# Chunked attention and two feed-forward layers on one core: first products in three sub-steps, one four-bank accumulator tile, a new order

## The chip, the cores and the metric

The engines are PE (matrix products, and PEld, its loading of the stationary operand), DVE (vector), ACT (scalar, with a table for exp), POOL (here mostly the issuer of outgoing transfers) and SP (issuer of all incoming transfers). Each engine works its instructions off in the order in which they stand and waits at semaphores for the others.

## The reference, cut to what matters

Attention: 4 batches, 8 heads, 768 positions, head size 64. A chunk of 32 queries sees 8 memory keys, 16 keys to the left, its own 32 and 8 to the right, 64 in all:

```python
scores = scale * np.matmul(q_c, k_full.transpose(0, 1, 3, 2))
scores = scores - np.max(scores, axis=-1, keepdims=True)
a = np.exp(scores)
a = a / (np.sum(a, axis=-1, keepdims=True) + 1e-09)
out[:, :, c_start:c_end] = np.matmul(a, v_full)
```

The 3072 tokens of 512 values then go through two layers of 512 -> 2048 -> 512:

```python
h = x @ w_in;  g = s * np.maximum(h, 0.0) ** 2 + b;               x = g @ w_out
h = x @ w_in;  g = np.maximum(h, 0.0) + alpha * np.minimum(h, 0.0);  y = g @ w_out
```

The weights come as 64-bit floats. Every product of the two layers is made of three: each operand is split into a high and a low part, and high x low, low x high and high x high are added up in PSUM.

## The kernel before, in words

**Tiles and blocks.** The tokens are 24 tiles of 128 (a tile is 128 positions of one batch, all heads) and 6 blocks of 512 (4 tiles). The hidden 2048 values are 16 slices `f` of 128. A **unit** is one layer, one block `j` and one slice `f`: step `g1` makes the hidden slice (12 products of 128x128 by 128x512 into bank `ph`), ACT and DVE apply the activation and split the result into `gh` and `gl`, and `g2` adds its part of the output into the four PSUM banks `po` (again 12 products). The first three slices of block 0 are done in two halves of 256 tokens (`HALVES`), so the first half can begin when two tiles of attention are done. `g2` of a unit stands two units (`LAG`) behind its `g1`.

**Order of the units.** Blocks 0 and 1 run first through slices 0 to `SEG`-1, put their sums by in DRAM (`spill`), then go through the other slices and add. So the early part needs only the first `SEG` weights for two blocks. After them come blocks 2 to 5, then layer 2, all slices at a time.

**Attention.** Per tile: scores (`scores`, products named `sc`, or `sp` where a tile's scores and the former tile's values share a step `products`), row maxima, exp, row sums, reciprocals and scaling on DVE and ACT (`softmax`), a turn by PE (`pt` or `turns`), a copy to SBUF (`aT`), the products with the values (`px`, `sp`), and the split into `xh` on ACT and `xl` on DVE. Tiles in `BY_HEAD` take exp head by head with the sum as a by-product of ACT, the others in one instruction with the sum on DVE. Tiles 0 to 3 (`ALONE`) use the `po` banks in pairs, tile 0 and 2 one pair, 1 and 3 the other; later tiles use the pair `pa`. A score or value product of 32 instructions in the program runs as 64 products in the trace.

**Weights.** `convert` turns the raw 64-bit words of slice `f` into two 32-bit parts: magnitude (ACT), clamp, shift, low, sign (DVE), high part (ACT), rest (DVE). Slices 0 and 1 are loaded and converted with the two matrices apart (`w0i`, `w0o`, ...).

**What sets the order.** All steps are handed to `Plan` with a cost, a rank and what they wait for; `Plan.order` lists them by time of a model of the engines, the loads and the fetching of PE's own instructions, and the instructions are emitted in that order. The model's constants and the tables at the head of the file (`FIRST_LOADS`: order of the first loads on SP; `TILE_RANKS`, `CONV_RANKS`, `STEPS`: ranks) decide only the order; nothing of them is executed. `Pace` models PE: its `BLOCK` is a block of 256 instructions that has to be fetched, `due` when the next one is there.

## Time and profile before

| what | value |
|---|---|
| three runs | 1143.62, 1147.26, 1149.77 us |
| the profiled execution's own time | 1147.76 us |
| its span, first to last instruction | 1146.0 us |
| PE busy | 1117.8 us (98%) |
| DVE, ACT, POOL busy | 607.9, 350.9, 28.8 us |
| mean granted clock of PE | 0.995 |
| DMA moved | 98.32 MB, mean 86 GB/s |

The page of the profile gives busy times, 40 slices of the span, the chain that ended last and the costliest groups; other views used are the waits of one engine (who waited for whom), the timeline (instructions in order of time, like ones merged, the idle time before each group in brackets) and the table of windows (busy time of each engine in a stretch, with the granted clock). A line number such as L605 is that of the kernel before; the kernel after has other numbers.

### The profile page before, as it was taken

The page shows a single profiled execution, that of the slowest core. Times are in us where ns is not written, and L with a number is a line of the kernel's source. Part 1 is how long each engine was busy: PE and PEld are TensorE (multiplying, and loading weights), DVE is VectorE, ACT ScalarE, POOL GpSimd, SP SyncE. Part 2 cuts the span into 40 slices and gives each one's busy share as a digit, 9 for nine tenths or more (in the row PEclk, how much of TensorE's full clock was granted, in tenths as well). Part 3 has the DMA queues.
Part 4 walks back from the last instruction along what each step waited for, and adds up shares of the span by engine and source line. Part 5 has one row for each costly group of instructions (what it writes and reads, how often), then busy time and mean ns, then how long its engine had stood idle before and what let it go on. Part 6 is the DMA issues. An engine that isn't in the chain of part 4 may idle for free.

```text
span 1146.0 us, 18300 instructions
## 1 busy us (share of the span) xinstructions
PE 1117.8 (98%) x7848; PEld 926.0 (81%) x7848; DVE 607.9 (53%) x942; ACT 350.9 (31%) x615; POOL 28.8 (3%) x58
## 2 busy tenths in 40 slices
PE   4799999999999999999999999999999999999998
PEld 4788888888888888888887788888888888888886
DVE  6796945454544445434799844434433434344333
ACT  5675734332223223224565311111111111111111
POOL 0000000000000000000000000000000000000000
PEclk9899999999999999999999999999999999999999
DMA  9918013423113113004557102002002002000000
GB/s 345 351 38 302 10 66 110 146 82 125 51 42 138 42 42 134 1 1 170 198 184 255 76 1 101 10 1 94 17 1 92 19 1 89 23 1 4 34 1 37
DMA packets 46241, 98.32 MB, mean 86 GB/s; under 512 B 4944, under 2 KB 4944, under 8 KB 46160
## 3 DMA queue, kind: packets, MB, share of 16 engines
q1 hardware_dynamic: 40320, 77.22, 19.4%
q0 software_dynamic: 5696, 19.93, 4.6%
q8 instruction: 61, 1.00, 0.4%
q14 instruction: 20, 0.16, 0.0%
q10 hardware_dynamic: 144, 0.01, 0.0%
HBM read 76.16 MB, written 20.97 MB: 85 GB/s over the span
## 4 chain that ended last, share of the span: by engine, by line
PE 49%; issue 42%; DMA 3%; DVE 3%; POOL 1%; ACT 1%; SPq 0%; POOLq 0%; DVEq 0%; ACTq 0%
PE ph L605 24%; PE po L666 22%; PE po L664 2%; DMA raw<-in_win_dram 1%; POOL x1d L703 1%; DVE a L309 1%; DMA spill<-os 1%; DVE a L314 1%; DMA qT<-in_qt_dram 0%; PE sp L488 0%; DMA qa<-in_qt_dram 0%; DMA vd<-in_vw_dram 0%; DVE w L327 0%; DVE gl L649 0%; DMA x1d<-o 0%
## 5 line engine op out<-in xcount | busy, mean ns | idle before, releaser
L605 PE MATMUL ph<-xh,w 128*128 128x512 f32 (+1 forms) x1560 | 509.7, 389 | 1.6 <-issue 0.9
L605 PEld LDWEIGHTS ph<-xh,w 128*128 128x128 f32 x1560 | 293.7, 189 | 61.7 <-DVE g L636 1.1
L605 PE MATMUL ph<-xl,w 128*128 128x512 f32 (+1 forms) x780 | 302.0, 387 | 0.0
L644 ACT ACTIVATE gh<-g 128x512 fp32r<-128x512 f32 (+1 forms) x195 | 121.7, 624 | 465.8 <-DVE g L636 385.2
L664 PE MATMUL po<-gh,w 128*128 128x512 f32 (+1 forms) x792 | 257.9, 387 | 0.2 <-DVE o L688 0.2
L666 PE MATMUL po<-w,gh 128*128 128x512 f32 x768 | 251.6, 389 | 0.5 <-DVE o L700 0.5
L649 DVE TENSOR_TENSOR gl<-g,gh 128x512 fp32r<-128x512 f32 (+1 forms) x195 | 133.1, 683 | 101.7 <-ACT gh L644 100.2
L631 DVE TENSOR_SCALAR g<-ph,cst_sb 128x512 f32<-128x512 f32 x96 | 72.0, 750 | 213.2 <-PE ph L605 213.1
L664 PEld LDWEIGHTS po<-gh,w 128*128 128x128 f32 x792 | 148.7, 189 | 30.1 <-DVE o L688 0.7
L605 PEld LDWEIGHTS ph<-xl,w 128*128 128x128 f32 x780 | 147.6, 189 | 28.6
L666 PEld LDWEIGHTS po<-w,gh 128*128 128x128 f32 x768 | 144.1, 188 | 31.0 <-DVE o L700 1.2
L664 PE MATMUL po<-gl,w 128*128 128x512 f32 (+1 forms) x396 | 152.1, 384 | 0.0
L666 PE MATMUL po<-w,gl 128*128 128x512 f32 x384 | 149.4, 389 | 0.0
L616 ACT ACTIVATE g<-ph 128x512 f32<-128x512 f32 (+1 forms) x99 | 57.8, 584 | 137.7 <-PE ph L605 134.2
L664 PEld LDWEIGHTS po<-gl,w 128*128 128x128 f32 x396 | 75.0, 189 | 14.1
L623 DVE TENSOR_TENSOR g<-g 128x512 f32<-128x512 f32 x48 | 33.2, 692 | 97.0 <-ACT g L616 96.9
L666 PEld LDWEIGHTS po<-w,gl 128*128 128x128 f32 x384 | 72.1, 188 | 14.9
L627 DVE TENSOR_SCALAR g<-g,cst_sb 128x512 f32<-128x512 f32 (+1 forms) x99 | 52.6, 531 | 42.6 <-ACT g L621 41.3
L636 DVE SCALAR_TENSOR_TENSOR g<-ph,g 128x512 f32<-128x512 f32 x96 | 66.3, 690 | 2.9
L296 ACT ACTIVATE a<-raw 128x1024 f32<-128x1024 f32 (+1 forms) x36 | 37.6, 1045 | 22.6 <-DVE w L327 14.3
L321 ACT ACTIVATE w<-a 128x1024 fp32r<-128x1024 f32 (+1 forms) x36 | 34.8, 967 | 31.2 <-DVE a L314 30.1
L327 DVE TENSOR_TENSOR w<-a,w 128x1024 fp32r<-128x1024 f32 (+1 forms) x36 | 39.5, 1100 | 1.2 <-ACT w L321 1.2
(83 smaller groups left out, 517.6 us busy)
## 6 DMA issues: line engine op xcount, KB each, us to landing
raw<-in_win_dram SPq DMA_DIRECT2D x64, 256.0 KB, 4.7
raw<-in_wout_dram SPq DMA_DIRECT2D x64, 256.0 KB, 5.3
x1d<-o POOLq DMA_DIRECT2D x24, 512.0 KB, 3.4
vd<-in_vw_dram SPq DMA_DIRECT2D x40, 256.0 KB, 4.1
kd<-in_kw_dram SPq DMA_DIRECT2D x20, 368.0 KB, 5.0
xh<-x1d SPq DMA_DIRECT2D x6, 1024.0 KB, 5.6
xl<-x1d SPq DMA_DIRECT2D x6, 1024.0 KB, 7.6
qT<-in_qt_dram SPq DMA_DIRECT2D x20, 256.0 KB, 3.9
```

Source lines behind the costliest of these rows:

```text
L296: nc.scalar.activation(out=temp["a"], in_=words(1).bitcast(F32), func=ACTF.Abs)
L321: nc.scalar.activation(out=w[:, :, 0, :], in_=temp["a"], func=ACTF.Copy)
L327: nc.vector.tensor_sub(out=w[:, :, 1, :], in0=temp["a"], in1=w[:, :, 0, :].bitcast(F32))
L605: nc.tensor.matmul(p, lhsT=w[:, a, kk * P:(kk + 1) * P], rhs=x[:, kk, cols], start=(i == 0), stop=(i == 3 * KD - 1))
L616: nc.scalar.activation(out=new_g(u), in_=ph.pop(u), func=ACTF.Relu)
L627: nc.vector.tensor_scalar(out=g, in0=g, scalar1=cst_sb[:, 0:1], scalar2=cst_sb[:, 1:2], op0=ALU.mult, op1=ALU.add)
L631: nc.vector.tensor_scalar(out=new_g(u), in0=ph[u], scalar1=0.0, scalar2=cst_sb[:, 2 + f:3 + f], op0=ALU.min, op1=ALU.mult)
L636: nc.vector.scalar_tensor_tensor(out=g, in0=ph.pop(u), scalar=0.0, in1=g, op0=ALU.max, op1=ALU.add)
L644: nc.scalar.activation(out=gh, in_=gt[u], func=ACTF.Copy)
L649: nc.vector.tensor_sub(out=gl, in0=gt.pop(u), in1=gh.bitcast(F32))
L664: nc.tensor.matmul(po[d][:, cols], lhsT=w[:, a, ds_], rhs=g, start=start, stop=stop)
L666: nc.tensor.matmul(po[d], lhsT=g[:, ds_], rhs=w[:, a, :], start=start, stop=stop)
```

## The change

**First products in three sub-steps.** `g1` takes a list of kinds, and whether it is the first and the last of its bank. For layer 0, blocks 0 and 1 and slices below `APART` = 6 it is planned as three steps of four products: high x high needs the high part of the weight and the tiles' `xh` alone, low weight x high needs the rest of the weight, high x low needs `xl`. All other units keep one step of twelve, ordered kind by kind per quarter as before.

**One accumulator tile.** The four `po` banks are one tile for the whole kernel, not a new tile for each segment and each lone tile; tiles 0 to 3 get a view of two of its banks, so maxima, subtraction and the two splits of such a tile are one instruction, not two.

**Order.** `SEG` goes from 7 to 8, tile 3 takes exp by head too, the tables of ranks and of first loads have new numbers, and the model's load rate and instruction fetch have new constants (a block is asked for 48 instructions into the one before).

```diff
-SEG = 7
+SEG = 8
 LAG = 2
 HALVES = 3
+APART = 6
...
-FIRST_LOADS = """q0 q1 w1i v0 q3 w0o q2 v2 w0i v1 w1o q4 v3 w2 w3 w4 v4 w6 q5 v7 q6 v5 q7 w5 w9 v6 w7 w8""".split()
+FIRST_LOADS = """q0 q1 w1i v0 q3 w0i q2 v1 w0o v2 w1o q4 w2 w3 q5 v3 w7 v5 w4 w6 q6 v7 v4 w5 v6 w9 w8 q7""".split()
...
-BY_HEAD = (1, 2, 4, 5, 6)
+BY_HEAD = (1, 2, 3, 4, 5, 6)
...
-STEPS = (28, 18, 18, 47, 43, 38)
+STEPS = (59, 89, 62, 132, 93, 79)
...
-    BLOCK, FIRST = 256, 184
+    BLOCK, FIRST, AHEAD = 256, 184, 48
...
+            if block >= 0 and into == self.AHEAD:
                 self.due[block + 1] = t + fetch(t)
...
-    RATE = 396e3
+    RATE = 382e3
...
-    FETCH = 2.7, 5.3
+    FETCH = 1.6, 5.1
...
+    po_all = psum.tile([P, KD, BLK], F32, name="po")
+    po = [po_all[:, d] for d in range(KD)]
...
         if i in ALONE:
-            return [psum.tile([P, 2, HP, D], F32, tag=f"po{2 * ALONE[i] + par}", name=name) for par in range(2)]
+            both = po_all[:, 2 * ALONE[i]:2 * ALONE[i] + 2].rearrange("p b (two a n) -> p b two a n", two=2, a=HP)
...
+        each = [(kk, a, (xh, xl)[b][n]) for kk in range(KD) for a, b in kinds]
+        for i, (kk, a, x) in enumerate(each):
+            nc.tensor.matmul(ph[u], lhsT=w[:, a, kk * P:(kk + 1) * P], rhs=x[:, kk, cols],
+                             start=first and i == 0, stop=last and i == len(each) - 1)
...
+        if layer == 0 and j < 2 and f < APART:
+
+            his = [x_hi[j * TPB + t] for t in range(cols.start // P, cols.stop // P)]
+            s = plan.add("PE", 4 * mm, rank, lambda: g1(u, ((0, 0),), True, False), his + [conv_high[f], id_, in_turn[0]],
+                         takes=("ph", ("ph", u)), count=8)
+            rest = [(((1, 0),), [conv_done[layer, 0, f]]), (((0, 1),), xs)]
+            for n_, (kinds, needs) in enumerate(rest if f == 0 else rest[::-1]):
+                s = plan.add("PE", 4 * mm, rank, lambda kinds=kinds, n_=n_: g1(u, kinds, False, n_ == 1), [s, *needs], count=8)
```

**What moves.** Three places matter for the prediction. In the rows, `x32` or `x4` is the number of like instructions in a row; 32 score or value products run as 64.

The first place is the start of ACT's list, before (lines of the kernel before):

```order
L727 DMA cst_sb<-in_cst_dram 128x18
L296 ACT_TABLE_LOAD
L296 ACTIVATE a<-raw 128x512
L433 ACTIVATE e<-e 128x512
L452 ACTIVATE e,rs<-sc,nm 128x64 x6
```

and now:

```order
L724 DMA cst_sb<-in_cst_dram 128x18
L435 ACT_TABLE_LOAD
L435 ACTIVATE e<-e 128x512
L301 ACTIVATE a<-raw 128x512
L454 ACTIVATE e,rs<-po,nm 128x64 x6
```

The exp of tile 0 (`e<-e`) stood behind the first weight's magnitude (`a<-raw`); it now stands ahead of it, and the table's loading is the exp's.

The second place is PE from tile 1's values on (`px<-aT,vd`), before:

```order
L488 MATMUL px<-aT,vd 64x32 x32
L401 MATMUL sp<-kd,qT 32x64 x32
L401 MATMUL sc<-kv,qa 32x64 x32
L605 MATMUL ph<-xh_74,w 128x256
L605 MATMUL ph<-xl_76,w 128x256
L605 MATMUL ph<-xh_74,w 128x256 x2
```

and now:

```order
L490 MATMUL po<-aT,vd 64x32 x32
L606 MATMUL ph<-xh_74,w 128x256 x4
L409 MATMUL po<-kv,qa 32x64 x32
L409 MATMUL sp<-kd,qT 32x64 x32
L606 MATMUL ph<-xh_74,w 128x256 x4
L468 MATMUL po<-ident,qa 128x128 x4
L606 MATMUL ph<-xl_76,w 128x256 x4
L606 MATMUL ph<-xh_74,w 128x256 x4
L490 MATMUL po<-qa,kv 64x32 x32
```

A third of unit 0's `g1` comes ahead of the scores of tiles 3 (`po<-kv,qa`) and 4 (`sp`), the other thirds behind them and between tile 2's turn and values.

The third place is PE around the step that makes the scores of tile 5 and the values of tile 4 (`sp<-kd,qT`, `sp<-aT,vd`), before:

```order
L488 MATMUL px<-qa,kv 64x32 x32
L466 MATMUL pt<-ident,qa 128x128 x4
L466 MATMUL turns<-ident,e 128x128 x4
L488 MATMUL px<-qa,kv 64x32 x32
L401 MATMUL sp<-kd,qT 32x64 x32
L488 MATMUL sp<-aT,vd 64x32 x32
L664 MATMUL po_751<-gh,w 128x256
```

and now:

```order
L661 MATMUL po<-gh,w 128x256 x2
L661 MATMUL po<-gl,w 128x256
L661 MATMUL po<-gh,w 128x256
L606 MATMUL ph<-xh_74,w 128x256 x4
L606 MATMUL ph<-xl_76,w 128x256 x4
L606 MATMUL ph<-xh_74,w 128x256 x4
L409 MATMUL sp<-kd,qT 32x64 x32
L490 MATMUL sp<-aT,vd 64x32 x32
L661 MATMUL po<-gh,w 128x256
```

Before, this step stood right behind tile 3's values and ahead of all of `g2` and of units 2 to 5. Now, between tile 3's values and it, stand 40 half-width products of `g1` (the last third of unit 2, all of units 3 to 5), 36 of `g2` (units 0 to 2) and a turn. The number of matrix products in the program is the same, 6312.

## The prediction

> **What bounds the kernel now.** I read the page first, then who PE waited for, then PE's timeline up to 85 us.

> ```profile
> span 1146.0 us, 18300 instructions
> ...
> PE 1117.8 (98%) x7848; PEld 926.0 (81%) x7848; DVE 607.9 (53%) x942; ACT 350.9 (31%) x615; POOL 28.8 (3%) x58
> ...
> PE   4799999999999999999999999999999999999998
> ```

> PE is busy for 98% of the span, and the idle 28.2 us lie in the first slice, the second and the last. The change removes no product, so the time can only move where PE stands still or runs slowly. The waits of PE, longest first:

> ```profile
> PE sc L401 <- DMA kd<-in_kw_dram: 6.7, 2, 4.6
> ...
> PE sp L401 <- ACT w L321: 1.7, 1, 1.7
> ...
> PE sp L488 <- ACT qa L471: 0.7, 1, 0.7
> PE pt L466 <- ACT xh L509: 0.7, 1, 0.7
> PE px L488 <- ACT aT L471: 0.7, 1, 0.7
> ...
> PE px L488 <- ACT qa L471: 0.3, 1, 0.3
> ...
> PE pt L466 <- DVE qa L475: 0.2, 1, 0.2
> ```

> All but the 0.7 at `qa` (it lies at 84 us) stand ahead of 44.6 us. With the "issue" waits below and a third small one for keys (0.3), they are 21.4 us there, and 22.1 with `qa`. The timeline shows three kinds:

> ```profile
> 7.82 1.17 PE L401 MATMUL sc<-kd,qT 64*32 64x64 f32 x64 [2.07 <-DMA kd<-in_kw_dram]
> 13.75 1.08 PE L466 MATMUL pt<-ident,e 128*128 128x128 f32 x4 [4.76 <-DVE e L475]
> ...
> 20.42 1.93 PE L488 MATMUL px<-aT,vd 64*64 64x32 f32 x64
> ...
> 25.29 0.92 PE L401 MATMUL sp<-kd,qT 64*32 64x64 f32 x44 [2.00 <-issue]
> ...
> 27.41 0.41 PE L605 MATMUL ph<-xl,w 128*128 128x256 f32 x1
> ...
> 31.28 0.40 PE L605 MATMUL ph<-xh,w 128*128 128x256 f32 x2 [0.85 <-issue]
> ...
> 38.49 0.85 PE L401 MATMUL sp<-kd,qT 64*32 64x64 f32 x64 [1.73 <-ACT w L321]
> 39.27 1.25 PE L488 MATMUL sp<-aT,vd 64*64 64x32 f32 x45
> 43.78 0.85 PE L488 MATMUL sp<-aT,vd 64*64 64x32 f32 x19 [3.25 <-issue]
> ...
> 49.84 0.28 PE L605 MATMUL ph<-xh,w 128*128 128x256 f32 x1
> ...
> 49.96 0.28 PE L605 MATMUL ph<-xl,w 128*128 128x256 f32 x1
> ...
> 57.55 0.86 PE L401 MATMUL sp<-kv,qa 64*32 64x64 f32 x64
> ...
> 59.41 0.39 PE L664 MATMUL po<-gh,w 128*128 128x256 f32 x1
> ```

> First, waits for operands. Second, three "issue" waits of 2.00, 0.85 and 3.25 us, 6.1 in all, in which nothing named is missing. Each product has its own weight load, so two instructions. Counted along PE's list, the three lie behind about 694, 950 and 1464 instructions: 256, then twice 256 apart. The page's DMA table says what comes in such pieces:

> ```profile
> q8 instruction: 61, 1.00, 0.4%
> ```

> 61 pieces in 1.00 MB, 16.4 KB each; 15,696 instructions of PE by 61 are 257. So PE waits here for the next block of its own instructions, and only where it runs through 256 faster than a block comes. A block came 6.0 us after the last (31.28 - 25.29); the last stall ended 5.3 us after PE had resumed at 38.49.

> [...]

> Third, the clock:

> ```profile
> 40.00:44.00 4.00, 0.74 (x28) 0.62 (x26) 0.87 (x3) 1.12 (x1) 0.00 (x0) 0.50 0.98 331
> 44.00:49.80 5.80, 5.80 (x42) 5.74 (x39) 3.38 (x7) 2.20 (x10) 0.00 (x0) 0.50 1.04 389
> 49.80:60.00 10.20, 10.20 (x199) 9.93 (x198) 9.19 (x16) 8.28 (x24) 0.00 (x0) 1.00 1.04 380
> 60.00:70.00 10.00, 10.00 (x63) 9.01 (x62) 9.86 (x17) 8.34 (x27) 0.00 (x0) 1.00 0.02 8
> 70.00:80.00 10.00, 10.00 (x164) 8.16 (x163) 10.00 (x14) 6.61 (x9) 0.00 (x0) 1.00 0.01 2
> 80.00:90.00 10.00, 9.29 (x103) 7.64 (x102) 9.97 (x17) 5.46 (x9) 0.00 (x0) 1.00 0.29 95
> 90.00:100.00 10.00, 10.00 (x46) 8.29 (x45) 9.70 (x12) 7.83 (x12) 0.68 (x1) 1.00 0.98 353
> ```

> After the waits the granted clock (third number from the right) is 0.50 from 40.0 to 49.8 us, and a half-width product takes 0.41 us in place of 0.28. The first products, at 27.41, are as slow; the clock rose at about 29.4, behind 4 us without a gap.

> **The change part by part.** The sum is made against the profiled execution: span 1146.0, own time 1147.76 us, 0.5 above the median of the three runs.

> *Tile 0's exp ahead of the first weight.* ACT and, in the last row, DVE before:

> ```profile
> 9.08 1.28 ACT L296 ACT_TABLE_LOAD   x1 [9.08 <-DMA raw<-in_win_dram]
> ...
> 10.94 0.61 ACT L433 ACTIVATE e<-e 128x512 f32<-128x512 f32 x1
> ...
> 17.50 0.66 ACT L509 ACTIVATE xh<-px 128x256 fp32r<-128x256 f32 x2 [0.92 <-PE px L488]
> ...
> 6.88 0.75 DVE L429 TENSOR_TENSOR e<-sc,m 128x256 f32<-128x256 f32 x2
> ```

> The subtraction ended at 7.63, but table and exp stood behind the first weight, which landed at 9.08. Now the table starts at about 7.4 and the exp ends near 9.3, 2.2 us sooner (10.94 + 0.61 before). Tile 1's maximum (0.7) comes into DVE's chain behind it, so tile 0's turn gains 1.5. Then ACT is fuller, since tile 1's exps come closer behind: I estimate waits of 1.1 for `aT` and 0.9 ahead of tile 2's scores (for tile 0's `xl`), in place of the two of 0.7. Tile 1's values end at 21.2, before 20.42 + 1.93 = 22.35. Gain 1.5 - 0.6 = 0.9.

> *First products in thirds.* The first third of unit 0 waits for tile 1's `xh`: 0.66 on ACT and two handovers of about 0.2, 1.1 us, where PE had other work before. Behind it queue the scores of tiles 3 and 4, and DVE's maxima behind those, so it is felt in full. Further on, tile 2 and 3 have four handovers (tile 3's turn, unit 2's weight, tile 3's values, tile 3's `xh`). Two of these cost 0.2 and 0.3 before; the nearest rows say 0.2 to 0.7 each: 0.8 to 2.8, and I take 1.6, so 1.1 more than the 0.5. Loss together 2.2.

> *Instruction blocks.* The count in the new order puts the block ends 16 products into tile 3's scores, at the start of tile 2's values, 44 into tile 3's values, and 28 into tile 5's scores. The block end before these lies 20 products into tile 2's scores, at about 18.3 (21.2 less 1.93 for tile 1's values and most of the scores). From there PE's rows make about 5.1 us to the first of the three, and 5.7 and 5.3 to the next two, against the 5.3 to 6.0 that a block needed: stalls of 0.2 to 0.9, 0 to 0.3 and 0.1 to 0.8, together 0.3 to 2.0, and I take 1.1. Ahead of the fourth stand the 76 half-width products of the third place, at 0.12 us each (49.84 to 49.96) over 9 us: no stall. So 6.1 becomes 1.1, gain 5.0 (4.1 to 5.8).

> *Tile 5's scores moved.* The 1.73 us at 38.49 go by the view to ACT, but that step had also to wait for tile 5's keys, which were far down the list of loads; behind 9 us of products both are there. Gain 1.7. What comes next in its place needs three weights and tile 3, counted above. SP's list hides nothing new: at 7.82 the first 1.28 MB were there, and at 389 GB/s (windows below) the values of tile 3, now 10.1 MB down, come at about 30.5, for use at 34.

> Idle before 85 us: 22.1, less 0.9, plus 2.2, less 5.0, less 1.7, less the 0.7 at `qa`, which hung on tile 7's order and which I count as gone: 16.0. That is 6.1 less.

> *The clock.* Without those stalls there is no second slow stretch. From 43.78 + 0.78 to 49.84 PE made 24 half-width products in 5.28 us; at 0.12 they take 2.88: 2.4. Tile 5's step took 2.04 (38.49 to 39.27 + 1.25) + 0.78 = 2.82 us of work, the next of its kind 59.41 - 57.55 = 1.86: 1.0. Gain 3.4. Against it, some 1.4 us of the idle time saved lie before 29.4, where work goes at about 0.12 / 0.22 of its speed: 0.6 of them count for nothing.

> [...]

> *At nothing:* the joined tile and two-bank views save four DVE instructions per lone tile (0.1 each) that PE does not wait for singly; tile 3 by head moves about 1.2 us from DVE to ACT, which is idle for 2 of 10 us there. The eighth slice changes no product, and the transfers are the same 98.32 MB in another order.

> Sum: -6.1 - 3.4 + 0.6 = **-8.9**. Span 1137.1, own time 1138.9; I say **1139 us**. The unknown costs reach 1.2 + 0.9 up, 0.8 + 0.8 down, and a late clock 3 up: 1136 to 1143 for this case.

> **The rivals.**

> *DVE becomes the bound.* For: from 60 to 100 us it is busy 9.86, 10.00, 9.97 and 9.70 of 10 (the third busy time in those rows), converting weights at 5 us each (three steps of 1.22, as in the rows below, and two shorter), and PE comes 8.9 us sooner. Against: its own idle time from 38 to 60 was

> ```profile
> 38.00:44.00 6.00, 2.84 (x5) 0.63 0.94 310
> 44.00:50.00 6.00, 3.58 (x7) 0.51 1.04 389
> ```

> 3.2 + 2.4 us there, and 10.2 - 9.2 = 1.0 to 60 (row above), 6.6 us, which waited for PE and now goes too. Then 8.9 - 6.6 = 2.3 us come back, 1141.2, and a little at each late weight: 1142.

> *The clock rises late.* For: the first products are now cut up by scores and turns, with waits of 1.1, 0.6 and up to 0.9 us around 22 to 32 us. Against: it rose at 29.4 behind a stretch of the same kind. Were it to rise only after such a stretch as from 40.0 to 49.8 has two thirds of, 6.5 us more of work run at 0.12 / 0.22: 3.0 lost, 1142.

> *It doesn't do what it says.* The issue waits are not blocks of instructions, and stay wherever they were: 5.0 + 3.4 come back, 1147. Against: the count in steps of 256.

> *Slower: the eighth weight.* With `SEG` at 8, unit 10 needs an eighth weight, where before block 1 began again with the first. The last steps of the seventh and eighth weight that DVE made, and unit 9's `g1` in the chain of waits:

> ```profile
> 77.63 1.22 DVE L327 TENSOR_TENSOR w<-a,w 128x1024 fp32r<-128x1024 f32 x1
> ...
> 82.43 1.22 DVE L327 TENSOR_TENSOR w<-a,w 128x1024 fp32r<-128x1024 f32 x1
> ```

> ```profile
> 79.57 2.73 PE ph L605 x12
> ```

> Unit 10 follows about 5 us behind unit 9's start, 84.5 then and 75.6 now. If DVE, full from 60 on, makes no weight sooner than before, the eighth is there at 83.65 and PE stands for 8.1 of the 8.9 us gained; a clock that then falls for another 9.8 us costs 4.5. That is 1147.8 - 0.8 + 4.5 = 1151.5, more if block 1's end is late too. It decides once DVE has won under 4 us; against it stand the 6.6.

> **How the numbers follow.** Forecast 0.62, DVE 0.12, late clock 0.11, not what it says 0.08, eighth weight 0.07. Range 1135.5 to 1146: the lower end is the sum with all unknowns at their best, the upper takes in DVE and the late clock together (1139 + 3 + 3) and leaves the last two out. Below 0.5% a measurement of this kernel can't be told from no change; that is 5.7 us, 1141.5 to 1153. Faster: nearly all of the forecast and a third of the two at 1142, 0.68; slower: most of the eighth weight, with block 1's end late too, 0.05; same 0.27.

> **What would show it.** In the profile after: the table loaded from about 7.4; no issue wait over 1 us and together about 1; no row of clock 0.50 between 40 and 50 us; tile 5's scores starting at about 46 without a wait; PE without a gap from 38 to 100 us; its idle total near 21 against 28.2. Wrong: an issue wait of 2 us or more, a wait for `w` (DVE, the rest of a weight) of over 1 us between 50 and 90, or slow products after 36.

## The result, and the profile after

The changed kernel takes **1189.79 us** (median of four runs, 1185.66 to 1192.92), against 1147.62 for the kernel before on the same chip. The ratio is 1.0381, 95% interval 1.0351 to 1.0411: slower by 42 us, where the forecast was 1139. The profiled execution took 1187.70 us with a span of 1185.9.

The page of the kernel after: the span, the busy times of the engines, and PE's busy tenths in 40 slices of the span.

```profile
span 1185.9 us, 18289 instructions
...
PE 1129.5 (95%) x7848; PEld 923.2 (78%) x7848; DVE 607.5 (51%) x930; ACT 352.4 (30%) x626; POOL 28.8 (2%) x58
...
PE   3899999999999998999999999999999999999997
```

PE's idle time is 1185.9 - 1129.5 = 56.4 us, twice the 28.2 of before, and PE is also busy 11.7 us longer with the same 7848 products. The tenths show hardly a hole: what was lost comes in pieces too small for a slice. Who PE waited for, longest sums first (total, times, longest):

```profile
PE po L663 <- DVE y L711: 8.4, 10, 0.9
PE po L661 <- DVE o L697: 6.0, 5, 1.4
PE po L409 <- DMA kd<-in_kw_dram: 4.6, 1, 4.6
...
PE po L663 <- ACT y L709: 3.4, 5, 0.7
PE po L468 <- ACT e L454: 3.3, 1, 3.3
PE po L661 <- ACT os L673: 3.1, 2, 2.4
...
PE po L490 <- ACT e L454: 2.5, 1, 2.5
...
PE po L409 <- ACT aT L473: 2.0, 1, 2.0
```

Of these rows only two have a counterpart before: the one for the keys (`kd`, 4.6 us) and the 3.3 us of tile 0's turn (4.8 before). For reads of `po` there were two waits before, of 0.5 and 0.2 us, both for `o`. L661 and L663 are `g2`; `os`, `o` and `y` are the reads by which ACT and DVE empty `po` at the end of a segment. A product into `po` now waits for a *read* of `po`. One such end, in the timeline of the kernel after:

```profile
1091.75 0.39 PE L663 MATMUL po<-w,gh 128*128 128x512 f32 x1
1092.18 0.60 ACT L709 ACTIVATE y<-po 128x512 f32<-128x512 f32 x1 [4.58 <-PE po L663]
...
1092.83 0.50 PE L663 MATMUL po<-w,gh 128*128 128x512 f32 x1 [0.69 <-ACT y L709]
...
1093.40 0.39 PE L663 MATMUL po<-w,gh 128*128 128x512 f32 x1
1093.88 0.69 DVE L711 COPY y<-po 128x512 f32<-128x512 f32 x1 [1.59 <-PE po L663]
...
1094.63 0.50 PE L663 MATMUL po<-w,gh 128*128 128x512 f32 x1 [0.84 <-DVE y L711]
```

Each quarter `d` of the output takes three products of a unit into its own bank. ACT's read of bank 0 begins at 1092.18, not when bank 0 is complete but when bank 1 is too (1091.75 + 0.39). The first product into bank 2, at 1092.83, then waits for that read, and the first into bank 3, at 1094.63, for the read of bank 1. Writer and readers take turns, although no two of them touch the same bank. From one product to the next PE needs 1.08 us (1091.75 to 1092.83) where 0.23 is usual.

The opening of the kernel after, PE alone:

```profile
7.53 1.18 PE L409 MATMUL po<-kd,qT 64*32 64x64 f32 x64 [1.76 <-DVE e L431]
12.02 1.09 PE L468 MATMUL po<-ident,e 128*128 128x128 f32 x4 [3.31 <-ACT e L454]
15.57 1.93 PE L490 MATMUL po<-aT,vd 64*64 64x32 f32 x64 [2.46 <-ACT e L454]
...
20.59 1.18 PE L409 MATMUL po<-kv,qa 64*32 64x64 f32 x64 [2.04 <-ACT aT L473]
21.71 1.93 PE L490 MATMUL po<-aT,vd 64*64 64x32 f32 x64
26.47 1.23 PE L606 MATMUL ph<-xh,w 128*128 128x256 f32 x4 [2.83 <-ACT xh L511]
```

At 7.53 the scores of tile 1 wait for DVE's subtraction of *tile 0*, at 15.57 the values of tile 0 for ACT's exps of *tile 1*: two tiles in different pairs of banks. The first of these waits cost next to nothing, since with a tile per bank (below) the same scores wait for their keys until 7.55; the second cost 1.6 us. Tile 1's values end at 21.71 + 1.93 = 23.64, later than before (22.35). Even so the stretch in which the kernel before had its slow clock is quick (the third number from the right is the granted clock):

```profile
40.00:44.00 4.00, 3.01 (x75) 2.50 (x76) 2.90 (x7) 4.00 (x13) 0.00 (x0) 1.00 0.53 185
44.00:49.80 5.80, 5.80 (x50) 5.63 (x48) 5.77 (x13) 4.19 (x12) 0.00 (x0) 1.00 0.91 277
...
106.80:110.20 3.40, 3.40 (x9) 2.66 (x8) 3.33 (x5) 0.13 (x1) 0.00 (x0) 0.50 1.05 395
```

The clock fell later instead, three times for 3.41 us (0.50 from 106.76, 198.92 and 553.91 us on), each behind such waits; the last row is the first of the three.

### The profile page after: what moved, and what is told of

Its sections match the earlier page's. It is cut to its first block, busy times and chain, and to the rows that moved or that the text cites. A ratio compares the mean times of both kernels' runs of the same rounds, so it can differ in the third digit from the quotient of the medians.

```text
span 1185.9 us, 18289 instructions
## 1 busy us (share of the span) xinstructions
PE 1129.5 (95%) x7848; PEld 923.2 (78%) x7848; DVE 607.5 (51%) x930; ACT 352.4 (30%) x626; POOL 28.8 (2%) x58
## 2 busy tenths in 40 slices
DMA packets 46241, 98.32 MB, mean 83 GB/s; under 512 B 4944, under 2 KB 4944, under 8 KB 46160
## 4 chain that ended last, share of the span: by engine, by line
PE 89%; DMA 4%; DVE 4%; ACT 2%; issue 1%; SPq 0%; DVEq 0%; ACTq 0%
PE ph L606 41%; PE po L663 22%; PE po L661 22%; DMA raw<-in_win_dram 2%; PE sp L490 2%; PE sp L409 1%; PE turns L468 1%; DVE o L697 1%; DMA spill<-os 1%; DMA kv<-in_kw_dram 1%; DVE y L711 1%; ACT o L693 0%; DMA raw<-in_wout_dram 0%; DMA o<-spill 0%; DVE gl L648 0%
## 5 line engine op out<-in xcount | busy, mean ns | idle before, releaser
L606 PE MATMUL ph<-xl,w 128*128 128x512 f32 (+1 forms) x780 | 295.6, 388 | 0.0
L661 PE MATMUL po<-gh,w 128*128 128x512 f32 (+1 forms) x792 | 262.3, 389 | 16.3 <-DVE o L697 6.0
L663 PE MATMUL po<-w,gh 128*128 128x512 f32 x768 | 256.2, 392 | 13.7 <-DVE y L711 8.4
L661 PEld LDWEIGHTS po<-gh,w 128*128 128x128 f32 x792 | 148.0, 188 | 52.4 <-DVE o L697 8.7
L663 PEld LDWEIGHTS po<-w,gh 128*128 128x128 f32 x768 | 144.1, 188 | 50.8 <-DVE y L711 12.7
L661 PE MATMUL po<-gl,w 128*128 128x512 f32 (+1 forms) x396 | 152.3, 385 | 0.0
L663 PE MATMUL po<-w,gl 128*128 128x512 f32 x384 | 149.6, 389 | 0.0
L661 PEld LDWEIGHTS po<-gl,w 128*128 128x128 f32 x396 | 74.4, 188 | 13.8 <-issue 0.2
L663 PEld LDWEIGHTS po<-w,gl 128*128 128x128 f32 x384 | 72.1, 188 | 14.4
```

What stands on the lines that cost most here:

```text
L606: nc.tensor.matmul(ph[u], lhsT=w[:, a, kk * P:(kk + 1) * P], rhs=x[:, kk, cols], start=first and i == 0, stop=last and i == len(each) - 1)
L661: nc.tensor.matmul(po[d][:, cols], lhsT=w[:, a, ds_], rhs=g, start=start, stop=stop)
L663: nc.tensor.matmul(po[d], lhsT=g[:, ds_], rhs=w[:, a, :], start=start, stop=stop)
```

## The experiments

Two theories stood against each other. *One tile*: as `po_all` is a single tile, the program's semaphores order every access to it against every other, whichever bank it touches. *The order*: thirds, eight slices and the new tables are themselves slower.

### The changed kernel with a tile per bank

```diff
-    po_all = psum.tile([P, KD, BLK], F32, name="po")
-    po = [po_all[:, d] for d in range(KD)]
...
+            if first:
+                po[d] = psum.tile([P, BLK], F32, tag=f"po{d}", name=f"po{d}")
```

with lone tiles in two one-bank tiles, as before the change. PE's list is the same product for product.

> The changed kernel with its order of instructions kept, but with po in one tile per bank again, taken anew in each segment, and with lone tiles in two one-bank tiles as before the change (so ten more DVE and four more ACT instructions in the opening). Theory 'one tile' (a write into any bank of po_all waits for reads of every other bank of it): the waits of PE for os, o and y between products into po go, idle time falls from 56 us to about 20, the clock stays up after its first rise, and the time is 1139 us, 1134 to 1146. Rival 'the order' (thirds, eight weights in the first segment and the new tables are themselves slower): the time stays at 1180 to 1190 us and the waits between products into po stay.

Measured: 1138.62 us (1138.00 to 1139.11), ratio to before 0.9938 (0.9916 to 0.9961); span 1136.2. All the waits for `y` are gone. The same end of a segment as above, PE, ACT and DVE:

```profile
1047.68 0.61 PE L669 MATMUL po<-w,gh 128*128 128x512 f32 x2
1048.10 0.60 ACT L715 ACTIVATE y<-po 128x512 f32<-128x512 f32 x1 [3.89 <-PE po L669]
1048.13 0.39 PE L669 MATMUL po<-w,gl 128*128 128x512 f32 x1
1048.36 0.61 PE L669 MATMUL po<-w,gh 128*128 128x512 f32 x2
```

ACT reads bank 0 from 1048.10 to 1048.70 while PE goes on into banks 1 and 2 in steps of 0.23 us. Neither takes longer for it: the read 0.60 us, as in the kernel after, where PE waits for it (1092.18), and the products 0.39 us each, 0.23 apart, as elsewhere.

As the order is the same, the two traces can be laid side by side. The kernel after is behind by 6.8 us once the lone tiles are through (and keeps that to 84 us), by 29.5 when the second layer begins, and by 49.7 at the end. In the second layer it loses 3.2 to 3.3 us at each of the first five ends of a block and 3.1 at the last. It comes in three steps of about 1.1 us: at the first product into bank 2, at the first into bank 3, and at the next block's first into bank 2. Of the 49.7, 35.5 are idle time (56.4 against 1136.2 - 1115.3 = 20.9) and 14.2 longer products: products slow up to about 31.7 us, not 24.8 (four half-width ones take 1.22 us at 30.50 and 0.73 at 33.32, with banks apart 1.22 at 21.55 and 0.74 at 24.98), three relapses of the clock, and the products that restart behind a wait, 0.50 instead of 0.39.

This is also the fastest of the versions here, 0.6% ahead of the kernel before.

### The kernel before with the one tile alone

```diff
+    po_all = psum.tile([P, KD, BLK], F32, name="po")
+    po = [po_all[:, d] for d in range(KD)]
...
-                po[d] = psum.tile([P, BLK], F32, tag=f"po{d}", name=f"po{d}")
```

> The kernel before with one edit: its four banks po0 to po3 are one tile of four banks, written and read through views; the lone tiles keep their two reads each, and the order of instructions stays. Theory 'one tile': each segment's end gains two to three waits of about 0.85 us of PE and the opening gains false waits between lone tiles, so idle time rises from 28 us to 65 or more and the time is 1185 to 1200 us. Rival 'the order': 1145 to 1150 us, as before.

Measured: 1189.32 us (1186.81 to 1191.35), ratio 1.0379 (1.0350 to 1.0408). The old order with the new tile loses as much as the change did. The idle time is 1185.0 - 1130.7 = 54.3 us, less than the 65 expected; here too a part of the loss is longer products, 12.9 us. The waits of PE:

```profile
PE po L665 <- ACT y L711: 6.9, 10, 0.7
...
PE po L663 <- DVE o L699: 6.0, 5, 1.4
PE po L468 <- ACT e L454: 4.9, 1, 4.9
```

So the tile is enough to cause the loss, and taking it away is enough to undo it. What is left is which accesses it holds up.

### Two tiles of two banks: pairs, and crossed

Pairs have banks 0 and 1 in one tile and 2 and 3 in the other:

```diff
-    po_all = psum.tile([P, KD, BLK], F32, name="po")
-    po = [po_all[:, d] for d in range(KD)]
+    po_two = [psum.tile([P, 2, BLK], F32, name=f"po{n}") for n in range(2)]
+    po = [po_two[d // 2][:, d % 2] for d in range(KD)]
```

> The changed kernel with two tiles of two banks each in place of the one of four: lone tiles keep their two-bank view and their single reads, the order stays. Theory 'one tile': of the three handovers at a segment's end (0 to 1, 1 to 2, 2 to 3) only the first and the last still wait, and the lone tiles of the two pairs no longer wait for each other; the loss after 100 us falls by about a third, to some 28 us, and the time is 1165 us, 1155 to 1175. Rival 'the order': 1180 to 1190 us.

Measured: 1151.08 us (1148.82 to 1155.38), ratio 1.0045 (1.0026 to 1.0065). Less was lost than expected, and not one wait for `y` is left. The expectation had the wrong handovers: it took bank 1's products to wait for the read of bank 0. But the order puts the read of bank `d` *behind* the products of bank `d` + 1, as the rows at 1091.75 and 1092.18 show; so it is bank 2 that waits for the read of bank 0, and bank 3 for that of bank 1. In pairs those never share a tile. That asked for the same two tiles crossed, 0 with 2 and 1 with 3:

```diff
-    po = [po_two[d // 2][:, d % 2] for d in range(KD)]
+    po = [po_two[d % 2][:, d // 2] for d in range(KD)]
```

> The changed kernel with two tiles of two banks each, as in the run with pairs, but slice 0 shares its tile with slice 2 and slice 1 with slice 3 (pairs: 0 with 1, 2 with 3); the order stays. Theory 'a product waits for the read that the order puts ahead of it in the same tile': the order puts the read of slice d behind the products of slice d + 1, so slice 2 waits for the read of slice 0 and slice 3 for that of slice 1. With pairs these never met in one tile, here they do: the waits for y come back in the second layer, some 0.2 to 0.5 us each with as much lost in the restart, and the time is 1154 us, 1146 to 1165. Rival 'the number of banks in a tile decides': as with pairs, 1151 us and no wait for y in the second layer.

Measured: 1145.68 us (1144.30 to 1146.68), ratio 1.0004 (0.9989 to 1.0019). The total was overestimated: crossed came out ahead of pairs, where it was expected behind. But the mechanism shows in the second layer. Laid beside the kernel with banks apart, crossed loses 0.7 to 0.8 us at each end of a block there, pairs nothing, one tile 3.1 to 3.3. No wait for `y` stands in the list of waits, since a read starts as soon as its own bank is full:

```profile
1055.04 0.60 ACT L709 ACTIVATE y<-po 128x512 f32<-128x512 f32 x1 [3.89 <-PE po L663]
1055.07 0.39 PE L663 MATMUL po<-w,gl 128*128 128x512 f32 x1
...
1055.30 0.90 PE L663 MATMUL po<-w,gh 128*128 128x512 f32 x2
```

The pair of products that spans banks 1 and 2 takes 0.90 us, with the second one held until the read ends, where 0.62 is usual. In the first layer pairs lose more than crossed: when the second layer begins, pairs are 12.4 us behind banks apart (631.82 against 619.42), with 8.0 us of waits for `os` and `o` and with slow products from 450.0 to about 457 (0.63 us each, 0.39 usual), and crossed 4.1 (623.56). There a product of the next segment waits for the read of the other bank of its pair (1.60 us at 349.48); with banks apart the same product, at 342.85, ran ahead of that read. Both let the opening end within 0.4 us of banks apart, so its 6.8 us came from the tiles of different pairs waiting for each other.

### One tile, emptied after the last bank

```diff
-            plan_finish(key, rank, parts)
+            plan_finish(key, rank, parts[-1:] * KD)
```

> The changed kernel with the one tile kept, but the reads that empty po at a segment's end come only after the last product into all four banks (the order of everything behind the first segment's end is worked out anew with that). Theory 'one tile': no product of the same segment is left behind a read, so the waits between products into po go and what remains is a wait of up to 2 us where the next segment's first product finds the four reads not done, partly covered by the first products of the next weight; 1145 to 1160 us. Rival 'the order': 1180 us or more.

Measured: 1153.15 us (1151.27 to 1155.88), ratio 1.0068 (1.0046 to 1.0090), idle time 1150.6 - 1118.5 = 32.1 us. The tile can be kept at a fraction of its price if every read stands behind every write of the segment (what follows the first segment was put in a new order with that). The waits of the opening, 1.8 to 3.3 us each, are as in the kernel after, and it stays 14.5 us behind banks apart.

### First products whole

The rest takes the kernel with banks apart (1138.62) and undoes one other part of the change in each.

```diff
-APART = 6
+APART = 0
```

> The changed kernel with banks apart (1138.6 us), and with the first products whole again instead of in thirds; the tables stay and the order of the opening is worked out anew with that. The prediction put the thirds down as a loss of 2.2 us of waits: by it the time is 1136 to 1138 us. Rival 'the thirds earn': a whole product must wait for the rest of its weight and tile, and what stands behind it waits too, 1141 us or more.

Measured: 1143.29 us (1142.48 to 1144.60), ratio to before 0.9980 (0.9964 to 0.9995). With the tables as they are, and the opening's order worked out for each, the thirds earn 4.7 us. Without them PE waits 1.6 us for an `xl` ahead of a `g2`, 1.6 for one ahead of a tile's scores and 1.4 for the rest of a weight (`w`), and the granted clock is 0.50 from 39.9 to 43.3 us.

With thirds for the first three slices only,

```diff
-APART = 6
+APART = 3
```

> The changed kernel with banks apart (1138.6 us), with only the first three weights' products in thirds (the six half-width units of the opening and unit 0 to 2 of block 1), those of weights 3 to 5 whole. If the thirds earn in the opening, where tiles come one by one, this keeps all of it: 1138 to 1140 us. If they earn where the weights of 3 to 5 come late, 1141 to 1144 us, as with all products whole (1143.3).

Measured: 1139.61 us (1138.76 to 1140.07), ratio 0.9940 (0.9922 to 0.9958). Nearly all of the gain lies in the first three slices: the half-width units of the opening and units 0 to 2 of block 1, which this run does not tell apart.

### Seven slices in the first segment

```diff
-SEG = 8
+SEG = 7
```

> The changed kernel with banks apart (1138.6 us), and with seven weights in the first segment of blocks 0 and 1 as before the change, instead of eight. The prediction put the eighth weight at nothing, or, as a rival, at a loss: 1137 to 1140 us by the forecast, 1135 or less if the eighth weight is late where eight are used. Rival 'the eighth weight earns': 1142 us or more.

Measured: 1147.58 us (1146.46 to 1150.13), ratio 1.0019 (1.0003 to 1.0036): 9 us more than with eight. To 70 us the two kernels run alike (PE busy for 55.7 us, with eight slices 54.8). Then the segment's end meets a turn in the bank pair `pa`, which by the view is released behind ACT's `os`, and the clock falls for 10.2 us:

```profile
82.70 0.95 PE L471 MATMUL turns<-ident,qa 128*128 128x128 f32 x4 [3.18 <-ACT os L679]
```

```profile
82.90:93.10 10.20, 8.47 (x82) 6.68 (x81) 4.54 (x5) 3.22 (x5) 1.76 (x3) 0.50 0.57 164
```

The tables are fitted to eight slices; that seven are slower as such is not shown, as the kernel before has seven and no such wait.

### Blocks of instructions, moved by 32 products

The kernel before, with half of tile 0's first scores made twice, in time that PE has to spare:

```diff
-        for hp in range(HP):
+        for hp in (0, 1, *range(HP)) if i == 0 else range(HP):
```

> The kernel before, in which tile 0 makes half of its first scores twice: 32 products more in the trace, 64 instructions, in a stretch in which PE then waits for tile 1's keys anyway; nothing else is changed. Theory 'instruction blocks of 256': the three issue waits move 32 products ahead of their old places: the first from 19 products into tile 4's scores to 51 into tile 1's values, the second from 2 products into unit 1 into the end of tile 3's scores, the third from 45 products into tile 4's values to 13 into them; their sum stays between 4 and 8 us and the time between 1143 and 1151 us. Rival 'something that PE waits for at these places': the waits stay at their old products.

Measured: 1145.41 us (1143.88 to 1147.60), ratio 1.0000 (0.9985 to 1.0015). The second issue wait did move 32 products ahead, into tile 3's scores:

```profile
24.94 1.30 PE L401 MATMUL sc<-kv,qa 64*32 64x64 f32 x51 [1.21 <-DVE xl L513]
26.74 0.46 PE L401 MATMUL sc<-kv,qa 64*32 64x64 f32 x13 [0.51 <-issue]
```

The first and third vanished, and another of 1.41 us came at 53.74, so the sum fell from 6.1 to 1.9, below the 4 to 8 expected. Counted as places in PE's list of products, the issue waits fall on the same few numbers in the kernels of this table, whatever work stands there:

```text
before              347  474       729
shifted by 32            475            984
after                    475
banks apart              474
old costs (below)   347  475  601       983
```

They are multiples of 128 products, 256 instructions, apart, to within 4. The step of 256 is shown; what decides whether a wait comes at such a place, and how long it is, is not. Over its runs the time did not gain the 4 us by which such waits fell (ratio 0.9985 to 1.0015): in the profiled one, 1.21 us for `xl` (row above) and slow products from 54.1 to about 57.4 us (a half-width one 0.41 us, 0.28 usual) came in place of a part. The step of tile 5's scores waited 2.0 us for keys in it, so the 1.73 put down to `w` before was, as the prediction had it, one of two things late there.

### The planner's costs alone

The kernel with banks apart, planned with the old constants of load and fetch (and without 1.2 us that the new model adds for the tenth load), and the kernel before, planned with the new ones. The edit of the first:

```diff
-    BLOCK, FIRST, AHEAD = 256, 184, 48
+    BLOCK, FIRST, AHEAD = 256, 184, 0
...
-    RATE = 382e3
+    RATE = 396e3
...
-    FETCH = 1.6, 5.1
+    FETCH = 2.7, 5.3
```

> The changed kernel with banks apart (1138.6 us), planned with the fetch and load costs of the kernel before (a fetch begins at a block's start and takes 2.7 or 5.3 us, 396 GB/s, no extra for the tenth load) and the new tables; the order comes out otherwise. The prediction's term 'instruction blocks' holds that block ends in the wrong places cost issue waits. By it: if the corrected costs matter, issue waits of 2 us or more are back and the time is 1142 to 1147 us; if they only trim what the tables set, 1138 to 1141 us with issue waits of 1 to 2 us.

Measured: 1146.01 us (1143.38 to 1148.79), ratio 0.9998 (0.9983 to 1.0013). The issue waits are back, 0.56, 1.68, 0.83 and 0.59 us. No single one is of 2 us, but the sum, 3.7 us, and the time are those of the first expectation. Beside them the first turn waits 5.25 us for tile 0's exp and comes at 14.33 (12.17 with the new costs), which is made good when tile 1's values end (20.6); but a later turn waits 2.2 us, and the products behind it are slow (four half-width ones take 1.20 us at 34.48, 0.74 at 38.99).

```profile
14.33 1.08 PE L471 MATMUL pt<-ident,e 128*128 128x128 f32 x4 [5.25 <-ACT e L457]
...
29.80 0.39 PE L610 MATMUL ph<-xl,w 128*128 128x256 f32 x1 [1.68 <-issue]
```

> The kernel before, planned with the corrected fetch and load costs, all tables and everything else as before. If the corrected costs alone take the block ends to better places, the issue waits fall from 6.1 us to 3 or less and the time to 1140 to 1144 us; if the tables do it, it stays at 1145 to 1149 us.

Measured: 1146.59 us (1145.21 to 1148.47), ratio 0.9999 (0.9988 to 1.0010). No issue wait of 0.1 us or more is left, and nothing is gained. PE waits for operands instead, and has its slow stretch 9 us later:

```profile
48.09 0.39 PE L606 MATMUL ph<-xh,w 128*128 128x256 f32 x1 [2.32 <-ACT g L617]
...
52.95 0.58 PE L665 MATMUL po<-gh,w 128*128 128x256 f32 x1 [2.41 <-ACT gh L645]
```

```profile
48.70:59.00 10.30, 7.89 (x125) 6.86 (x124) 8.13 (x15) 7.36 (x20) 0.00 (x0) 0.50 1.05 384
```

The gain needs the new costs and the rest of the change together.

## Why the prediction was wrong, point by point

**The step that failed** is "*At nothing:* the joined tile and two-bank views save four DVE instructions per lone tile". The edit was costed as a saving of instructions on DVE (over the four tiles it is ten on DVE and four on ACT: 930 against 940 and 626 against 630 with banks apart), and what the one tile does to the order between engines was not asked: a product now waits for reads of other banks. Alone on the kernel before it costs 42 us (ratio 1.0379), and the change without it takes 1138.62. None of the five cases, the slower rival among them, had this mechanism. It could have been asked of the profile of before, where at a segment's end ACT reads one bank while PE writes the next, without a wait:

```profile
1057.85 0.60 ACT L712 ACTIVATE y<-po 128x512 f32<-128x512 f32 x1 [3.89 <-PE po L666]
1057.88 0.39 PE L666 MATMUL po<-w,gl 128*128 128x512 f32 x1
1058.10 0.62 PE L666 MATMUL po<-w,gh 128*128 128x512 f32 x2
```

Any ordering between the banks must put waits there, at the 14 ends of segments. An estimate from the reads of before: two or three of 0.6 to 0.7 us make 1.2 to 2.1 us an end, 17 to 29 us in all, without handovers and the clock. Measured, against banks apart, it was 3.1 to 3.3 us an end in the second layer, and 49.7 - 6.8 = 42.9 us in all after the opening.

The other steps describe the kernel with banks apart, and there they can be read one by one. PE's rows of its opening:

```profile
12.17 1.09 PE L471 MATMUL pt<-ident,e 128*128 128x128 f32 x4 [3.45 <-DVE e L480]
...
18.74 1.93 PE L493 MATMUL px<-aT,vd 64*64 64x32 f32 x64
21.55 1.22 PE L610 MATMUL ph<-xh,w 128*128 128x256 f32 x4 [0.88 <-ACT xh L514]
...
26.45 0.63 PE L471 MATMUL pt<-ident,qa 128*128 128x128 f32 x4 [0.72 <-DVE nm L447]
...
28.57 0.40 PE L610 MATMUL ph<-xh,w 128*128 128x256 f32 x2 [0.77 <-issue]
...
32.20 0.63 PE L471 MATMUL pt<-ident,qa 128*128 128x128 f32 x4 [0.82 <-DVE qa L480]
...
37.03 1.25 PE L610 MATMUL ph<-xh,w 128*128 128x256 f32 x8 [0.76 <-ACT xh L514]
...
45.86 0.86 PE L406 MATMUL sp<-kd,qT 64*32 64x64 f32 x64
```

- *Tile 0's exp ahead of the first weight*: its turn comes at 12.17, 1.58 us sooner (1.5 forecast); tile 1's values end at 20.67 (21.2).
- *First products in thirds*: the first third waits 0.88 (1.1). Of the four handovers named, two wait, tile 3's turn and its `xh`: 0.82 + 0.76 = 1.6 (1.6). Tile 2's turn, which was not named, adds 0.72, so the loss is 0.88 + 1.58 + 0.72 - 0.5 = 2.7 (2.2). As a sum of waits against the order before it was about right. As a price of the thirds it misled: whole products with these tables cost 4.7 us more.
- *Instruction blocks*: one issue wait of 0.77 in place of 6.1 us; the forecast was 1.1. It lies two products ahead of tile 2's values, where the second of the three was counted. (By the trace the third of before lies behind 729 products, 1458 instructions, not 1464.)
- *Tile 5's scores moved*: at 45.86 without a wait (about 46); the 0.7 for `qa` is gone.
- *The clock*: once up, it stays up (1.00 in every stretch from 30 to 200 us, mean 0.999 over the span). That the products would become quick 4.5 us sooner, at about 24.8, was not foreseen: four half-width ones take 1.22 us at 21.55 and 0.74 at 24.98. The first rise is read from the products alone, here as in the forecast: in the kernel before their step falls from 0.21 to 0.12 us at 29.4, while the column of the granted clock reads 1.00 from 24 us on. The products gain 1117.8 - 1115.3 = 2.5 us in all (3.4 - 0.6 = 2.8), a part of that by the early rise; that the term agrees is partly luck.
- *Idle total*: 20.9 us (near 21), and the span 1136.2 (1137.1).
- *The eighth slice at nothing*: right for the transfers (98.32 MB), and no weight came late; but with this order's tables seven slices cost 9 us.

In the kernel after itself, the signs named for the opening held where the tile was not in the way: the table is loaded at 7.54, the only issue wait is 0.27 us, no clock of 0.50 between 40 and 50. Three signs failed: the idle total of 56.4, tile 5's scores, without a wait but at 52.65 and not 46, and PE without a gap from 38 on (0.31 and 0.69 us at 42.10 and 43.53). Of the signs named for "wrong", neither issue waits of 2 us nor waits for `w` came; slow products after 36 did, in the three relapses from 106.8 on, but no sign pointed at `po`.

**The rivals.** *It doesn't do what it says* falls with the places of the issue waits. *DVE becomes the bound* and *the eighth weight* do not show: with banks apart the timeline names no wait of PE between 38 and 97 us. The opposite of *the clock rises late* came true there. In the kernel after the first products did stay slow longer, to about 31.7; as the order is the same, that is the one tile's doing and not that of the cut-up products.

## What to carry to other kernels

Where several buffers become views of one tile, list who writes one part while another engine reads the next, at every place where the tile is used and not only where the views are wanted: in these runs ordering goes by the tile. Here each such handover cost about 1.1 us of PE in the second layer, and all of it, with the opening and the clock, 49.7 us. A saving of a few instructions on an engine that PE hardly waits for did not pay for that. And a stall that is taken away is worth only what the next thing in line lets through: 6.1 us of issue waits gone brought nothing in one order, and 5.3 us less of them were part of a gain of some 7 us in another.

## What the runs showed of the hardware that was not expected

**The clock fell behind short waits.** In the kernel after, PE waited 0.79 us at 196.86 and 0.78 at 198.62; each took about 1.2 us from one product's start to the next. The next 3.4 us are slow:

```profile
195.50:198.90 3.40, 1.83 (x7) 0.92 (x6) 2.17 (x4) 1.97 (x4) 0.00 (x0) 1.00 0.00 0
198.90:202.30 3.40, 3.40 (x11) 2.74 (x11) 1.47 (x3) 0.93 (x2) 1.08 (x2) 0.50 0.48 189
202.30:205.70 3.40, 3.40 (x16) 2.78 (x15) 0.02 (x1) 1.23 (x2) 0.00 (x0) 0.99 0.68 228
```

PE was busy for 1.83 of 3.40 us, and 3.40 slow us followed. Waits of 0.69 and 0.84 us at 551.88 and 553.68 had the same behind them, 0.50 from 553.91 to 557.32. Waits of the same 0.69 and 0.84 us at 1092.83 and 1094.63 left the clock at 1.00, as it is from 560 to 1185 us, over all the ends in the second layer. So the length of a wait alone does not decide it in this kernel; what does is not shown. The slow stretches are not of one length either: 3.41 us three times here, about 6.8 from 450.2 on with pairs, 10.2 from 39.6 on in the kernel before and from 82.9 on with seven slices.

**PE stood still at steps of 256 instructions.** The step holds over the kernels of the table above, with waits of up to 3.25 us. The trace has the other half of it too: in the kernel before, pieces of the queue `q8 instruction` (16.4 KB each) move at 22.9, 28.7 and 41.5 us, and the three issue waits end at 25.29, 31.28 and 43.78, 2.2 to 2.6 us after them; in the kernel after one moves at 32.2, and its issue wait ends at 34.68. No issue wait follows the pieces at 33.6 and 47.6 in the kernel before, or at 37.3 and 41.3 in the kernel after.
